# Attention ahead of two MoE layers: four raw buffers, one rotary table, and a start time of its own for every step

## The chip, the cores and the metric

The kernel runs on one core of one Trainium2 chip. The metric is device time in microseconds (us) from launch to end; three runs of the kernel before gave 1014.96 us as their median (1010.65 to 1017.69).

## The reference, cut to what matters

Inputs are q, k and v of shape (4, 8, 576, 64): 4 batches, 8 heads, 576 positions, 64 features, all float32.

- Attention: q and k are turned by rotary tables (`x1*cos - x2*sin`, `x1*sin + x2*cos`), `scores = q_rot @ k_rot.T / 8`, a softmax over the keys (row maximum taken off, exponent, division by the row sum), times v. The result is x with 2304 rows of 512.
- First layer: `h = x @ w_in`, ELU of h, `x = g @ w_out` (2048 hidden columns).
- Second layer: `out = ((x @ w1) * (x @ w2)) @ w3 @ w_out` (1024 hidden columns).

## The kernel before

Attention is done in 16 **units**, one for each batch and pair of heads. The two heads of a unit lie in partitions 0 to 63 and 64 to 127. A TensorE product at float32 accuracy is made of three products of rounded parts (`PAIRS`): a tensor is kept as a high part `hi` and a rest `lo`.

The steps of a unit and the codes that the order uses for them:

- **L1, L0, Lv** (`load`, `load_v`, lines 269 to 275): the loads of k, q and v, issued by SyncE (SP). k and q each come as one tile of 128 x 1152 floats (576 KB): the values and the same values with the two feature halves exchanged. The tiles lie in the pool `qk` (line 237), which has 3 buffers.
- **Km, Ka, Kh, Kl** with w = 1 for k and 0 for q: `turned` multiplies a tile by its table (line 278, GpSimd, POOL), `added` sums its two halves (line 281, POOL), `hi_of` makes the high part (line 289, through line 89, ScalarE, ACT), `lo_of` the rest (line 293, POOL). A raw buffer comes free after Kl.
- **D** (`diagonal`, line 298): two small DMAs that copy the last 64 queries of each head into one tile.
- **SA0 to SA3, SB0 to SB3** (`scores`, line 342): six matmuls each, 128 queries of head A or B against 576 keys. **SC** (`last_scores`, lines 355 to 361): the last 64 queries of both heads in one, with small matmuls of the unit before. Scores lie in PSUM, in a pool of 2 slots (`ps_s`).
- **m** (`maximum`, line 369, VectorE, DVE) and **e** (`exponent`, line 379, ACT): row maximum and exponent of one block. A slot of scores comes free after its e.
- **T, Z** (`turns`, `side_turns`, `last_turns`, lines 390, 410, 420): 88 transposes of 64 x 64 a unit on TensorE (PE), and **E** (lines 426, 428): their copies out of PSUM by ACT or DVE.
- **n, sp, r4** (lines 446 to 454): reciprocals of the sums on DVE, spread by POOL, wanted by the transposes of line 410 and the matmuls of line 356.
- **P0 to P4** (`weigh`, lines 466, 474): the products with v, and **w** (line 486): their normalised result into x.
- **f, W0 to W3** (`fetch_w`, line 103; `weight_step`, lines 499 to 505): 16 tiles of the first layer's weights are fetched (512 KB each) and rebuilt by ACT and DVE.

Work that prepares the first layer (sums of weights, the first splits of x and of a weight set) stands in the last units: `first_sum`, `early_x`, `first_pair`. `early_x` and `first_pair` issue their POOL and ACT steps in one go.

**What sets the order.** All of this lies under a schedule written out by hand. `TIMES` gives each code an offset, unit u takes `u * PERIOD + offset`, `steps` spreads the matmuls of a step by a small distance, and all events are sorted by `max(t, first)` (lines 556 to 648). Only the order counts: each engine runs its own instructions in that order, and each instruction starts when what it depends on is done. Events of the first units that would lie before time zero are clamped (`first=1.75` for L, K and D, zero for the others) and so keep their order among themselves. Two rules follow from the offsets: on SP, D of unit u comes ahead of k of unit u + 2, a weight tile, and q of unit u + 1; on POOL, k of unit u + 2 is turned ahead of q of unit u + 1.

Before the events stands a prologue (lines 621 to 641): the first table and the first tiles of unit 0 in eight pieces on SP (`first_load`, lines 300 to 309; two runs of 288, 128 or 448 floats for each partition), then k of unit 1, `idt`, v of unit 0, and, as the first events, three weight tiles, all ahead of q of unit 1. Unit 0 is turned and split by DVE and ACT (`first_part`). The table of q is loaded on its own and scaled by 1/8 on ACT (line 640). Thirty matmuls on a zero tile keep PE busy while the loads come (`warm_up`).

After attention a planner orders the first layer (`Plan`, lines 668 to 716; products in line 737, lines 780 and 781) by costs and due times of its own, and a fixed loop the second (line 1211 and on).

Of the kernel before, what the change touches and what calls it, by code (L numbers as in the profile page):

```python
# [18 lines left out]
P = 128  # L19
SCALE = 1.0 / 8.0  # L20
# [5 lines left out]
PERIOD = 13.879  # L26
HALF_T = 0.07
TIMES = {
# [12 lines left out]
}  # L41
FIRST_LOADS = ((1, "L1"), (1, "L0"), (2, "L1"))
WARM = 30
# [3 lines left out]
SUM_AT = (7.2, 11.2)  # L47
SWITCH_AT = 15.05
X_AT = (15.06, 15.25, 15.45, 15.65)
PAIR_AT = (15.35, 15.85)  # L50
# [16 lines left out]
def kernel(  # L67
# [161 lines left out]
    with ExitStack() as c1:  # L229
# [7 lines left out]
        qk_p = pool0("qk", 3)  # L237
# [11 lines left out]
        tab = tab_p.tile([P, 2, 2, S], F32, name="tab")  # L249
# [19 lines left out]
        def load(u, w):  # L269
            raws[u, w] = qk_p.tile([P, 2, S], F32, tag="raw_qk", name="raw_qk")  # L270
            nc.sync.dma_start(raws[u, w], (q, k)[w][units[u][0], units[u][1]])
# [4 lines left out]

        def turned(u, w):
            pool.tensor_tensor(raws[u, w], raws[u, w], tab[:, w], op=ALU.mult)  # L278
# [9 lines left out]
        def hi_of(u, w):  # L288
            copy_hi(hl_of(u)[:, w, 0], raws[u, w][:, 0], act)

        def lo_of(u, w):
            hl = hls[u]
            pool.tensor_tensor(hl[:, w, 1], raws[u, w][:, 0], hl[:, w, 0].bitcast(F32), op=ALU.subtract)  # L293

        def diagonal(u):
            for j in range(2):
                h = ROWS[j]
                nc.sync.dma_start(diag[u % 2][h, :, h].bitcast(F32), hls[u][h, 0, :, 512:S].bitcast(F32))

        def first_load():  # L300
            for w in (1, 0):
                raws[0, w] = qk_p.tile([P, 2, S], F32, tag="raw_qk", name="raw_qk")
            for dst, src, a, b in (
                (tab[:, 1], tables[:, 1], 0, 288), (raws[0, 1], k[0, 0], 0, 288),
                (tab[:, 0], tables[:, 0], 0, 128), (raws[0, 0], q[0, 0], 0, 128),
                (tab[:, 1], tables[:, 1], 288, S), (raws[0, 1], k[0, 0], 288, S),
                (tab[:, 0], tables[:, 0], 128, S), (raws[0, 0], q[0, 0], 128, S),
            ):
                nc.sync.dma_start(dst[:, :, a:b], src[:, :, a:b])

        def first_part(w, a, b):
            r, hl, s = raws[0, w], hl_of(0), (SCALE, 1.0)[w]

            def turn(z):
                dve.tensor_tensor(r[:, z, a:b], r[:, z, a:b], tab[:, w, z, a:b], op=ALU.mult)

            def add():
                dve.tensor_tensor(r[:, 0, a:b], r[:, 0, a:b], r[:, 1, a:b], op=ALU.add)

            def high():  # L320
                copy_hi(hl[:, w, 0, a:b], r[:, 0, a:b], act, s)

            def low():
                hi, lo = hl[:, w, 0, a:b].bitcast(F32), hl[:, w, 1, a:b]
                if w:
                    dve.tensor_tensor(lo, r[:, 0, a:b], hi, op=ALU.subtract)
                else:
                    dve.scalar_tensor_tensor(lo, r[:, 0, a:b], s, hi, op0=ALU.mult, op1=ALU.subtract)

            return [lambda: turn(0), lambda: turn(1), add, high, low]  # L330
# [18 lines left out]
        def last_scores(u):  # L349
# [9 lines left out]
            for n in range(2):  # L359
                for i, (a, e) in enumerate(PAIRS):  # L360
                    pe.matmul(
                        s[:, n, :288], diag[u % 2][:, a], hls[u][:, 1, e, n * 288:(n + 1) * 288],
# [3 lines left out]
        def maximum(u, c, j):  # L366
            nm = sm_p.tile([P, 1], F32, tag="nm", name="nm")
            S_t[u, c, j, "m"] = nm
            dve.tensor_reduce(nm, S_t[u, c, j][:, :, :288], axis=AX.XY, op=ALU.max, negate=True)  # L369

        def exponent(u, c, j):
# [3 lines left out]
            else:  # L375
# [4 lines left out]
                p_.rearrange("p (n i) -> p n i", n=2), S_t[u, c, j][:, :, :288], ACTF.Exp,  # L380
# [143 lines left out]
        def first_pair(q):  # L524
            t = set_slot()
            set_pair(0, q, t)
            src = (whole(("i", 0)), sums_of[0][0])[q]
            high_of(t, src)
            rest_of(t, src, pool)

        def early_x(k):
            xf_sum(0, k, pool)
            xf_high(0, k)
            xf_rest(0, k, pool)
# [21 lines left out]
        for code, t_ in TIMES.items():  # L556
            eng = {"a": act, "d": dve}[code[-1]] if code[0] == "E" else None
            for u in range(NU + 3):
                t = u * PERIOD + t_
                if code[0] == "S" and code[1] in "AB":  # L560
                    c = int(code[2])
                    if IN(u):
                        steps(t, scores(u, c, "AB".index(code[1])), 0.133)
                elif code == "SC":
                    if u <= NU:
                        event(t, last_scores, u)
                elif code[0] == "T":
                    du, c = HOST[int(code[2])]
                    if IN(u + du):
                        steps(t, turns(u + du, c, int(code[1])), HALF_T)  # L570
                elif code[0] == "Z":
                    c, l = int(code[2]), int(code[1])
                    v_ = u - (c < 3)
                    if IN(v_):
                        steps(t, last_turns(v_, l) if c == 2 else side_turns(v_, int(c == 1), l), HALF_T)
                elif code[0] == "P":
                    c = int(code[1])
                    v_ = u - (0, 0, 1, 1, 2)[c]
                    if IN(v_):
                        event(t, weigh, v_, c)  # L580
                elif code[0] == "m" and IN(u):
                    event(t, maximum, u, int(code[1]), int(code[2]))
                elif code[0] == "e" and IN(u):
                    event(t, exponent, u, int(code[1]), int(code[2]))
                elif code[0] == "E" and IN(u):
                    f, args = {
                        "X": lambda: (turned_out, (u, int(code[2]), 0)), "Y": lambda: (turned_out, (u, int(code[2]), 1)),
                        "Z": lambda: (side_out, (u, int(code[2]), int(code[3]))), "C": lambda: (last_out, (u, int(code[2]))), "4": lambda: (side4_out, (u,)),
                    }[code[1]]()
                    event(t, f, *args, eng)  # L590
                elif code[0] == "w" and IN(u) and (u, code) != (NU - 1, "w2"):
                    event(t, weighed, u, int(code[1]))
                elif code[0] == "n" and IN(u):
                    event(t, norm, u, *((0, 4), (4, 9))[int(code[1])])
                elif code[:2] == "sp" and IN(u):
                    event(t, spread, u, int(code[2]))
                elif code == "r4" and IN(u):
                    event(t, spread4, u)
                elif code[0] == "W" and u < len(PRE):
# [813 lines left out]
```

## Time and profile before

| | |
|---|---|
| median of 3 runs | 1014.96 us |
| the profiled execution | 1014.97 us |
| span of its instructions | 1013.2 us |
| PE busy | 964.7 us (95%) |
| DVE busy | 758.6 us (75%) |
| ACT busy | 652.1 us (64%) |
| POOL busy | 200.1 us (20%), nearly all in the first 30% of the span |
| mean granted PE clock | 0.979 |

The span runs from the first instruction to the last; the profiled execution has 1.77 us more than that around it. Busy PE is not PE at its peak: the ends of matmuls are modelled, and two that overlap count once.

### The profile page before, as it was taken

The numbers are of one execution on the slowest core, as the hardware profiler recorded it, in microseconds if no ns is written. First come the engines' busy times: TensorE is split into PE (matmuls) and PEld (weight loads), VectorE is DVE, ScalarE is ACT, GpSimd is POOL, SyncE is SP. The second block draws the span as 40 slices with busy tenths as digits, with TensorE's granted clock in tenths as the row PEclk, the third lists the DMA queues.
The fourth block names the chain that finished last, engine by engine and source line by source line (L and its number), as shares of the span: only waits on it lengthen the run. The fifth ranks groups of instructions, "written<-read, shape, count | busy, mean of one in ns | idle before, by whom it ended". The sixth has DMA issues, their size and how long they took to land.

```text
span 1013.2 us, 20015 instructions
## 1 busy us (share of the span) xinstructions
PE 964.7 (95%) x7692; PEld 870.4 (86%) x7692; DVE 758.6 (75%) x1463; ACT 652.1 (64%) x1406; POOL 200.1 (20%) x168
## 2 busy tenths in 40 slices
PE   4599999989989999999999999999999999999998
PEld 3477787878868999999999998998899999999997
DVE  4377777868858999999889999774747576676544
ACT  1477777867867778888778877774544354444432
POOL 1768687777450000000000000000000000000000
PEclk8599999999999999999999999999999999999999
DMA  7242424252410454657564576534142243224311
GB/s 246 86 157 104 170 92 172 96 164 90 156 51 1 141 171 152 218 181 240 192 198 157 191 232 228 179 102 138 40 130 74 73 144 90 84 74 135 90 36 63
DMA packets 65775, 135.19 MB, mean 133 GB/s; under 512 B 11280, under 2 KB 20624, under 8 KB 65680
## 3 DMA queue, kind: packets, MB, share of 16 engines
q1 hardware_dynamic: 65680, 133.92, 40.7%
q8 instruction: 60, 0.98, 0.4%
q14 instruction: 35, 0.29, 0.1%
HBM read 107.15 MB, written 25.69 MB: 131 GB/s over the span
## 4 chain that ended last, share of the span: by engine, by line
PE 75%; POOL 8%; DMA 8%; DVE 3%; ACT 2%; issue 2%; SPq 1%; POOLq 0%; DVEq 0%; ACTq 0%
PE y L780 13%; PE A L1211 10%; PE A L737 9%; PE o L1237 9%; PE B L1211 7%; PE B L737 7%; PE yb L781 7%; PE w L1141 4%; DMA raw_qk<-q_ 4%; POOL raw_qk L278 4%; DMA raw_qk<-k_ 3%; PE o L466 3%; PE s L342 2%; POOL raw_qk L281 1%; POOL hl L293 1%
## 5 line engine op out<-in xcount | busy, mean ns | idle before, releaser
L780 PE MATMUL y<-g,wo 128*128 128x512 f32 x576 | 204.1, 392 | 0.0
L781 PE MATMUL yb<-g,wo 128*128 128x256 f32 x576 | 161.2, 280 | 0.0
L342 PE MATMUL s<-hl 64*128 64x288 f32 x768 | 134.6, 323 | 24.6 <-ACT pr L379 24.3
L369 DVE TENSOR_REDUCE nm<-s 128x1 f32<-128x576 f32 x144 | 108.6, 755 | 62.8 <-PE s L342 50.2
L342 PEld LDWEIGHTS s<-hl 64*128 64x128 f32 x768 | 109.5, 194 | 43.6 <-ACT pr L379 31.7
L148 DVE TENSOR_TENSOR set<-set 128x512 fp32r<-128x512 f32 (+1 forms) x160 | 98.2, 619 | 43.8 <-ACT set L145 43.7
L780 PEld LDWEIGHTS y<-g,wo 128*128 128x128 f32 x576 | 107.8, 187 | 20.5
L379 ACT ACTIVATE pr<-s,nm 128x576 f32<-128x576 f32 x144 | 106.7, 741 | 25.8 <-DVE nm L369 23.9
L1211 PE MATMUL A<-xc,set 128*128 128x384 f32 x576 | 116.1, 336 | 0.2
L737 PE MATMUL A<-xf,set 128*128 128x384 f32 x552 | 111.2, 336 | 1.0 <-DVE p L797 0.9
L1237 PE MATMUL o<-W,g 128*128 128x512 f32 x432 | 111.1, 393 | 0.0
L1211 PEld LDWEIGHTS A<-xc,set 128*128 128x128 f32 x576 | 102.4, 188 | 7.8 <-DVE p L1298 1.0
L781 PEld LDWEIGHTS yb<-g,wo 128*128 128x128 f32 x576 | 108.7, 189 | 0.0
L737 PEld LDWEIGHTS A<-xf,set 128*128 128x128 f32 x552 | 93.7, 188 | 4.3 <-DVE p L797 1.3
L89 ACT ACTIVATE g<-p 128x384 fp32r<-128x384 f32 x48 | 25.2, 526 | 107.8 <-DVE p L1298 71.5
L278 POOL TENSOR_TENSOR raw_qk<-raw_qk,tab 128x1152 f32<-128x1152 f32 x30 | 79.3, 2646 | 66.7 <-DMA raw_qk<-k_ 52.4
L145 ACT ACTIVATE set<-set 128x512 fp32r<-128x512 f32 (+1 forms) x160 | 89.5, 568 | 3.7 <-DMA set<-kept 3.4
L1237 PEld LDWEIGHTS o<-W,g 128*128 128x128 f32 x432 | 80.0, 188 | 12.7
L1211 PE MATMUL B<-xc,set 128*128 128x384 f32 x432 | 86.5, 334 | 0.0
L737 PE MATMUL B<-xf,set 128*128 128x384 f32 x420 | 84.3, 336 | 0.0
L1211 PEld LDWEIGHTS B<-xc,set 128*128 128x128 f32 x432 | 75.9, 188 | 0.0
L737 PEld LDWEIGHTS B<-xf,set 128*128 128x128 f32 x420 | 72.6, 188 | 1.0
(214 smaller groups left out, 1914.0 us busy)
## 6 DMA issues: line engine op xcount, KB each, us to landing
set<-kept SPq DMA_DIRECT2D x120, 256.0 KB, 2.7
raw<-w_ SPq DMA_DIRECT2D x32, 512.0 KB, 4.3
kept<-wr SPq DMA_DIRECT2D x40, 256.0 KB, 3.2
raw_qk<-k_ SPq DMA_DIRECT2D x15, 576.0 KB, 4.2
raw_qk<-q_ SPq DMA_DIRECT2D x15, 576.0 KB, 6.4
raw<-w_in_ SPq DMA_DIRECT2D x16, 512.0 KB, 4.8
raw<-w_out_ SPq DMA_DIRECT2D x16, 512.0 KB, 4.8
w<-kept SPq DMA_DIRECT2D x24, 256.0 KB, 3.5
```

The source lines that it names most:

```text
L145: act.activation(t[:, 0, :w], t[:, 1, :w].bitcast(F32), ACTF.Copy)
L148: eng.tensor_tensor(t[:, 1, :w], t[:, 1, :w].bitcast(F32), t[:, 0, :w].bitcast(F32), op=ALU.subtract)
L278: pool.tensor_tensor(raws[u, w], raws[u, w], tab[:, w], op=ALU.mult)
L342: pe.matmul(S_t[u, c, j][:, n, :288], hl[h, 0, a, c * P:c * P + P], hl[h, 1, e, n * 288:(n + 1) * 288], start=(i == 0), stop=(i == 2),)
L369: dve.tensor_reduce(nm, S_t[u, c, j][:, :, :288], axis=AX.XY, op=ALU.max, negate=True)
L379: act.activation(p_.rearrange("p (n i) -> p n i", n=2), S_t[u, c, j][:, :, :288], ACTF.Exp, bias=S_t.pop((u, c, j, "m")), accum_out=sums[u ...
L737: pe.matmul(banks[b][:, :HF], set_w(n, k, a, c), x[:, e, c], start=(start and i == 0), stop=i == 5, skip_group_check=True,)
L780: pe.matmul(y_t[p, o], w_, g[:, c, :512], start=s, stop=t, skip_group_check=True)
L781: pe.matmul(yb_t[p, o // 2][:, o % 2], w_, g[:, c, 512:], start=s and o % 2 == 0, stop=t, skip_group_check=True,)
L1141: pe.matmul(ps, w3_t[i, j // 4][:, a, j % 4 * P:j % 4 * P + P], wo[j][:, c], start=(j == 0 and n == 0), stop=(j == 7 and n == 2), skip_gro ...
L1211: pe.matmul(ps[:, :HB], w[:, a, c * P:(c + 1) * P], x[:, c, b], start=(start and i == 0), stop=i == 5, skip_group_check=True,)
L1237: pe.matmul(outs[p, o], g[:, a, o % 3 * P:o % 3 * P + P], wW[f][:, c], start=(f == 0 and i == 0), stop=(f == NG - 1 and i == 2),)
```

## The change

- `qk` has 4 buffers in place of 3.
- Inputs q, k and the table are laid out in memory by halves: for each partition the first 288 positions of both parts, then the last 288, so that a half of a tile is one run of 2304 bytes. Tiles have the shape `[P, 2, 2, 288]` (half, part, position). `added`, `hi_of` and `lo_of` read one part as two runs of 288.
- One table is loaded in place of two (the queries of the second head are now in the rotated order of the keys, so `scores` shifts its columns by 64 for it and `diagonal` takes the first 64 columns of it). The table of q is made from it by one ACT instruction (`tab0`).
- `first_load`: the two halves of the table are issued by ACT, the halves of q and k by SP. Then follow k of unit 1, `idt`, q of unit 1, v of unit 0, one weight tile, and k of unit 2. Weight tiles two and three come after L0 of unit 2.
- `first_part`: q of unit 0 is multiplied and summed by POOL, k by DVE. An exponent on one column at the very start is ACT's first instruction after its two DMAs.
- `TIMES`, `PERIOD`, the clamp and the fixed places of the last steps give way to `STARTS`, a list of times for each code, one per unit. `early_x` and `first_pair` are cut into their single steps (`x`, `y`), `first_sum` too (`b`). Eight copies out of PSUM change sides between ACT and DVE, four and four of the same sizes.
- 26 matmuls in the warm-up in place of 30.

Transposes, matmuls, vector and scalar instructions keep their number and sizes otherwise.

```diff
-PERIOD = 13.879
-HALF_T = 0.07
-TIMES = {
-    "L1": -38.79, "f": -38.18, "Km1": -35.79, "L0": -22.65, "Km0": -18.40, ...
...
+HALF_T = 0.063
+STARTS = {
...
+    "SA0": dict(enumerate((8.98, 21.23, 36.65, 51.41, 65.37, 79.70, 94.04, ..., 208.73, 223.59), 0)),
+    "SB0": dict(enumerate((8.98, 22.75, 37.38, 52.04, 66.10, 80.44, ...), 0)),
+    "SA1": dict(enumerate((11.73, 25.47, 39.87, 54.16, 68.55, 82.88, ...), 0)),
+    "D": dict(enumerate((12.00, 21.83, 34.05, 46.48, 57.95, 72.65, 86.98, ...), 0)),
+    "L0": dict(enumerate((13.20, 21.23, 33.45, 45.88, 59.75, 74.45, 88.78, ...), 2)),
+    "L1": dict(enumerate((19.83, 32.05, 43.78, 59.15, 73.85, 88.18, ...), 3)),
+    "Km1": dict(enumerate((9.57, 25.69, 33.69, 45.88, 58.78, 72.99, 87.33, ...), 1)),
+    "Km0": dict(enumerate((13.92, 21.23, 38.21, 50.00, 61.44, 75.65, 89.99, ...), 1)),
+    "Kl0": dict(enumerate((19.78, 31.99, 44.43, 55.58, 71.19, 85.53, ...), 1)),
+    "Z11": dict(enumerate((25.47, 39.83, 54.16, 68.55, 82.88, ...), 1)),
+    "T12": dict(enumerate((13.36, 26.68, 42.32, 56.65, 71.04, 85.37, ...), 0)),
+    "y0": dict(enumerate((227.21, 248.85), 0)),
+    "y1": dict(enumerate((231.25, 250.13), 0)),
...
 }
-FIRST_LOADS = ((1, "L1"), (1, "L0"), (2, "L1"))
-WARM = 30
+WARM = 26
...
-        qk_p = pool0("qk", 3)
+        qk_p = pool0("qk", 4)
...
-            pool.tensor_tensor(raws[u, w][:, 0], raws[u, w][:, 0], raws[u, w][:, 1], op=ALU.add)
+            (dve if (u, w, "a") in ON_DVE else pool).tensor_tensor(raws[u, w][:, :, 0], raws[u, w][:, :, 0], raws[u, w][:, :, 1], op=ALU.add)
...
-            copy_hi(hl_of(u)[:, w, 0], raws[u, w][:, 0], act)
+            copy_hi(halves(hl_of(u)[:, w, 0]), raws[u, w][:, :, 0], act)
...
         def first_load():
             for w in (1, 0):
-                raws[0, w] = qk_p.tile([P, 2, S], F32, tag="raw_qk", name="raw_qk")
-            for dst, src, a, b in (
-                (tab[:, 1], tables[:, 1], 0, 288), (raws[0, 1], k[0, 0], 0, 288),
...
-                nc.sync.dma_start(dst[:, :, a:b], src[:, :, a:b])
+                raws[0, w] = qk_p.tile([P, 2, 2, HS], F32, tag="raw_qk", name="raw_qk")
+            for n in range(2):
+                nc.scalar.dma_start(tab[:, 1, n], tables[:, n])
+                for w in ((0, 1), (1, 0))[n]:
+                    nc.sync.dma_start(raws[0, w][:, n], (q, k)[w][0, 0, :, n])
...
-                    S_t[u, c, j][:, n, :288], hl[h, 0, a, c * P:c * P + P], hl[h, 1, e, n * 288:(n + 1) * 288],
+                    S_t[u, c, j][:, n, :HS], hl[h, 0, a, c * P + 64 * j:c * P + 64 * j + P], hl[h, 1, e, n * HS:(n + 1) * HS],
...
-        def early_x(k):
-            xf_sum(0, k, pool)
-            xf_high(0, k)
-            xf_rest(0, k, pool)
+        def early_x(k, s):
+            if s == 0 or s == 1 and k < 2:
+                xf_sum(0, k, pool)
+            if s == 1:
+                xf_high(0, k)
+            elif s == 2:
+                xf_rest(0, k, pool)
...
+        first_load()
+        pool.memset(zero, 0.0)
+        act.activation(warm[:, :1], zero[:, 0], ACTF.Exp)
+        for s_ in sums:
+            pool.memset(s_[:, :, 1:], 1e-9)
+        load(1, 1)
+        nc.sync.dma_start(idt, ident)
+        load(1, 0)
+        load_v(0)
+        fetch_w(PRE[0], w_in[PRE[0][1]])
+        load(2, 1)
```

## Rows read from the trace of the kernel before

**Rows 1.** Stages: us, engines' busy us (instructions), granted clock, DMA share, GB/s.

```profile
9.79:49.51 39.72, 15.50 (x111) 13.05 (x110) 13.32 (x23) 12.51 (x26) 22.09 (x13) 0.57 0.43 157
49.51:263.47 213.96, 201.13 (x3102) 169.85 (x3102) 165.38 (x324) 165.18 (x389) 156.70 (x124) 0.99 0.38 129
263.47:278.66 15.19, 15.19 (x242) 13.00 (x242) 12.76 (x25) 12.61 (x30) 4.50 (x6) 1.00 0.61 193
278.66:311.19 32.53, 27.81 (x391) 22.78 (x390) 16.62 (x34) 18.35 (x43) 15.16 (x13) 0.95 0.12 39
```

**Rows 2.** Chain that ended last, at 8 and at 104 us: start, us, what.

```profile
7.77 7.78 DMA raw<-w_in_
...
104.19 6.80 DMA raw_qk<-q_
```

**Rows 3.** Timeline, unit 0: start, us, engine, line; idle before and its releaser.

```profile
19.01 1.34 SPq L298 DMA_DIRECT2D diag<-hl  x2
...
20.40 0.59 SPq L271 DMA_DIRECT2D raw_qk<-k_  x1
24.74 5.18 POOL L278 TENSOR_TENSOR raw_qk<-raw_qk,tab 128x1152 f32<-128x1152 f32 x2 [8.73 <-issue]
...
31.42 0.68 ACT L89 ACTIVATE hl<-raw_qk 128x576 fp32r<-128x576 f32 x1 [15.23 <-POOL raw_qk L281]
...
32.88 3.16 PE L342 MATMUL s<-hl 64*128 64x288 f32 x12 [20.70 <-ACT pr L379]
```

**Rows 4.** Waits from 0 to 270 us: us in total, times, longest.

```profile
POOL raw_qk L278 <- DMA raw_qk<-k_: 52.4, 14, 11.0
...
PEld z L410 <- POOL rb L93: 14.9, 13, 2.8
```

**Rows 5.** PE timeline from 250 to 265 us, first rows of its groups.

```profile
250.73 0.40 PE L342 MATMUL s<-hl 64*128 64x288 f32 x1
...
252.48 0.69 PE L466 MATMUL o<-pT,v__3218 128*64 128x64 f32 x16
...
253.22 0.27 PE L390 MATMUL x<-idt,pr 64*128 64x64 f32 x1
...
254.62 1.09 PE L466 MATMUL o<-pT,v__3520 128*64 128x128 f32 x16
...
258.84 0.40 PE L342 MATMUL s<-hl 64*128 64x288 f32 x1
...
260.79 1.09 PE L466 MATMUL o<-pT,v__3821 128*64 128x128 f32 x16
261.81 0.66 PE L355 MATMUL s<-idt,pr 128*128 128x64 f32 x4
...
263.47 0.40 PE L342 MATMUL s<-hl 64*128 64x288 f32 x1
...
264.46 1.09 PE L466 MATMUL o<-pT,v__3821 128*64 128x128 f32 x16
```

**Rows 6.** The page's costliest groups: busy us, mean ns of one, idle before.

```profile
L369 DVE TENSOR_REDUCE nm<-s 128x1 f32<-128x576 f32 x144 | 108.6, 755 | 62.8 <-PE s L342 50.2
...
L379 ACT ACTIVATE pr<-s,nm 128x576 f32<-128x576 f32 x144 | 106.7, 741 | 25.8 <-DVE nm L369 23.9
```

**Rows 7.** POOL instructions by tile: ns min/median/max, first and last start.

```profile
L278 POOL TENSOR_TENSOR raw_qk<-raw_qk,tab x30: 2609/2644/2736, 13.3 to 258.3; 128x1152 f32<-128x1152 f32 x30
L281 POOL TENSOR_TENSOR raw_qk<-raw_qk x30: 1396/1423/1453, 30.0 to 262.6; 128x576 f32<-128x576 f32 x30
...
L200 POOL TENSOR_TENSOR xf<-xT,xf x2: 1832/1839/1846, 280.7 to 283.4; 128x768 fp32r<-128x768 f32 x2
```

**Rows 8.** Single microseconds, columns as in the stages above.

```profile
5.00:6.00 1.00, 1.00 (x11) 1.00 (x10) 0.45 (x2) 0.48 (x1) 0.00 (x0) 1.00 0.93 253
...
15.00:16.00 1.00, 0.00 (x0) 0.00 (x0) 0.00 (x0) 0.62 (x2) 1.00 (x1) 0.60 1.02 410
49.00:50.00 1.00, 1.00 (x13) 0.82 (x14) 0.38 (x1) 0.33 (x1) 0.00 (x0) 0.83 0.00 0
```

More of the change, by code (lines that the diff above doesn't have):

```diff
@@ L275, in load_v, with halves @@
             nc.sync.dma_start(vs[u], v[units[u][0], units[u][1]])
+        def halves(x):
+            return x.rearrange("p (n i) -> p n i", n=2)
         def turned(u, w):
-            pool.tensor_tensor(raws[u, w], raws[u, w], tab[:, w], op=ALU.mult)
+            (dve if (u, w, "m") in ON_DVE else pool).tensor_tensor(raws[u, w], raws[u, w], tab[:, w], op=ALU.mult)
         def added(u, w):
-            pool.tensor_tensor(raws[u, w][:, 0], raws[u, w][:, 0], raws[u, w][:, 1], op=ALU.add)
+            (dve if (u, w, "a") in ON_DVE else pool).tensor_tensor(raws[u, w][:, :, 0], raws[u, w][:, :, 0], raws[u, w][:, :, 1], op=ALU.add)
         def hl_of(u):
@@ L317, in add, with first_part, turn @@
+        def first_part(w, n, eng):
+            r, s = raws[0, w][:, n], (SCALE, 1.0)[w]
+            hi, lo = (hl_of(0)[:, w, e, n * HS:(n + 1) * HS] for e in range(2))
+            def turn():
+                eng.tensor_tensor(r, r, tab[:, 1, n], op=ALU.mult)
             def add():
-                dve.tensor_tensor(r[:, 0, a:b], r[:, 0, a:b], r[:, 1, a:b], op=ALU.add)
+                eng.tensor_tensor(r[:, 0], r[:, 0], r[:, 1], op=ALU.add)
             def high():
-                copy_hi(hl[:, w, 0, a:b], r[:, 0, a:b], act, s)
+                copy_hi(hi, r[:, 0], act, s)
@@ L323, in low @@
             def low():
-                hi, lo = hl[:, w, 0, a:b].bitcast(F32), hl[:, w, 1, a:b]
                 if w:
-                    dve.tensor_tensor(lo, r[:, 0, a:b], hi, op=ALU.subtract)
+                    dve.tensor_tensor(lo, r[:, 0], hi.bitcast(F32), op=ALU.subtract)
                 else:
-                    dve.scalar_tensor_tensor(lo, r[:, 0, a:b], s, hi, op0=ALU.mult, op1=ALU.subtract)
-            return [lambda: turn(0), lambda: turn(1), add, high, low]
+                    dve.scalar_tensor_tensor(lo, r[:, 0], s, hi.bitcast(F32), op0=ALU.mult, op1=ALU.subtract)
@@ L332, in slot_of @@
+            return dict(m=turn, a=add, h=high, l=low)
         def slot_of(u, c, j):
@@ L554, in steps @@
                 event(t + i * dt, f)
[L556 to L599, printed above, removed]
-                    event(t, weight_step, u, int(code[1]))
-                elif code[0] == "K" and 0 < u < NU:
-                    w = int(code[2])
-                    event(t, {"m": turned, "a": added, "h": hi_of, "l": lo_of}[code[1]], u, w, first=1.75)
-                elif code == "D" and 0 < u < NU:
-                    event(t, diagonal, u, first=1.75)
-                elif code[0] == "L" and 0 < u < NU:
-                    if (u, code) not in FIRST_LOADS:
-                        event(t, *((load_v, u) if code[1] == "v" else (load, u, int(code[1]))), first=1.75)
-                elif code == "f" and u < len(PRE):
-                    event(t, lambda u=u: fetch_w(PRE[u], (w_in, w_out)[PRE[u][0] == "o"][PRE[u][1]]))
@@ new lines, in each, with runs @@
+        def each(code, f, lo=0, hi=NU):
+            for u, t in STARTS[code].items():
+                assert lo <= u < hi
+                event(t, f, u)
+        def runs(code, f, dt):
+            for u, t in STARTS[code].items():
+                steps(t, f(u), dt)
+        for c in range(4):
+            for j in range(2):
+                runs(f"S{'AB'[j]}{c}", lambda u: scores(u, c, j), 0.133)
+                runs(f"T{j}{c}", lambda u: turns(u + HOST[c][0], HOST[c][1], j), HALF_T)
+                if c:
+                    runs(f"Z{j}{c}", lambda u: last_turns(u - 1, j) if c == 2 else side_turns(u - (c < 3), int(c == 1), j), HALF_T)
@@ new lines @@
+        event(min(min(v_.values()) for c, v_ in STARTS.items() if c[0] in "xy") - 0.001, switch)
+        parts = {}
+        one.enter_context(tc.manual_schedule())
+        first_load()
[9 more added lines that the diff above has]
+        load(2, 1)
@@ new lines @@
+        dve.memset(warm, 0.0)
+        warm_up(WARM)
+        for d in diag:
+            copy_hi(d, zero.to_broadcast([P, 2, P]), pool)
+        pool.memset(mask, 0.0)
+        for h in ROWS:
+            pool.memset(mask[h, h], 1.0)
+        event(STARTS["tab0"][0], lambda: act.activation(tab[:, 0], tab[:, 1], ACTF.Copy, scale=SCALE))
+        event(STARTS["two"][0], lambda: pool.tensor_tensor(two, idt[:, :D], idt[:, D:], op=ALU.add))
+        events.sort(key=lambda e: e[:3])
+        for *_, f, args in events:
+            f(*args)
@@ L1369, in turned, with by_half @@
         return np.ascontiguousarray(x).reshape(B, 4, P, 2, S)
-    def last_first(x):
+    def by_half(x):
         x = x.copy()
         x[..., 64:, :, :] = np.concatenate([x[..., 64:, :, 512:], x[..., 64:, :, :512]], axis=-1)
-        return x
+        x = x.reshape(*x.shape[:-1], 2, S // 2)
+        return np.ascontiguousarray(x.swapaxes(-3, -2))
     def values(x):
```

244 lines of the change are left out of this document (180 added, 64 removed), and 12 rows, old and new, of the table TIMES.

## The prediction

> **What bounds the kernel now.** I read the stages first [rows 1], because the change touches attention alone. Unit 0 takes 39.72 us, the next 13 units 213.96 / 13 = 16.46 each, unit 14 takes 15.19, and unit 15 with the way into the first layer 32.53. From 311.19 on, 702.0 us of the span are matmuls of the two layers; what they multiply stays the same, so I carry them over whole.
>
> Next came the chain of waits, to see who sets the pace where PE is not full. In unit 0 it goes from a weight tile that took 7.78 us to land [rows 2] through its rebuilding to the wait of SP, and on the timeline of that unit the rest can be followed [rows 3]: D of unit 0 is issued only at 19.01, k of unit 2 queues behind it (20.40), and POOL, whose order has k of unit 2 ahead of q of unit 1, starts that pair at 24.74. ACT stands before the high part of unit 1 until 31.42 with ready exponents behind it, and PE comes back at 32.88 after 20.70 us without work. That is a queue order, not a lack of an engine.
>
> In the 13 middle units the chain crosses the load of q, 6.80 us from its issue [rows 2]. POOL waited 52.4 us in 14 times for the loads of k, and PE's transposes waited 14.9 us in 13 times for a small POOL instruction that stood behind a multiplication without data [rows 4]: 1.15 a unit, nearly all of 16.46 - 15.19 = 1.27. Unit 14 has no more tiles to prepare; PE is busy all its 15.19 us [rows 1]. So 15.19 is what PE alone needs with this order.
>
> **The change, part by part.** The written start times are read for the order alone; every time below is from rows.
>
> *First scores.* DVE's first piece now starts in the sixth microsecond, when 590 kB (a piece of table and one of k) have landed, with the queues at 253 GB/s in runs of 1152 bytes; longer runs moved 410 GB/s [rows 8]. 590 kB at 253 GB/s are 2.3 us, which leaves 3.2 us of start and landing. The first scores now need the table's halves, q's first and k's two: 1.47 MB, 3.6 us at the fast rate, 5.8 at the slow one, so 6.8 to 9.0. Multiplication, sum, high part and rest follow, about 2.1 us (estimate: two on 576 and two on 288 columns, by 755 ns for 576 [rows 6]). That is 8.9 to 11.1 against 9.79; 2304 bytes lie between the two lengths of run, and I take 9.8, no gain. Issue from two queues is worth at most the 0.6 us that an issue takes [rows 3], and the DMA engines are 93% busy in that second [rows 8].
>
> The Trainium skill (DMA: Bandwidth & Descriptors, section "Issuing engines are not separate DMA queues") says that transfers started by several engines share the same 16 DMA engines and that only the time of initiating them is saved; by it the second queue would give nothing beyond that issue, and the 93% agree.
>
> *Unit 0.* It is now bound by its two slots of scores: six matmuls, maximum, exponent, then the slot is free. Six matmuls take 0.99 to the next group's first [rows 5], then come 0.755 and 0.741 [rows 6] and some 0.2 for the hops between engines (estimate): 2.7 for each of four pairs, then SC, 1.66 from 261.81 to 263.47 [rows 5]. Sum 12.5. POOL prepares unit 1 meanwhile: q of unit 0 (all landed at 7.5 to 10.2, then 2.1), two multiplications of 2.64, four instructions of 1.42 [rows 7], small ones: ready at 21 to 24, when unit 0 ends. What covers the loads is that all four tiles of units 0 and 1 are issued before the first weight tile and before D; if that failed, the 20.70 us [rows 3] would come back in part.
>
> *PE's clock.* PE is idle about a third of unit 0 (four pairs of 1.75 and an SC of 1.66 in 12.5). After the idle stretch from 12.2 us on the granted clock fell to 1.2 GHz within the sixteenth microsecond, and it came back to 2.4 only in the fiftieth [rows 8], though PE had work from 32.88 on: gaps keep it low. I expect a fall in unit 0 and a return in unit 1, which is full. At half speed the 0.99 of a slot's matmuls grows by some 0.6 (estimate, a part of it is latency), in four pairs 2.5; and some 4 us of unit 1 at half speed, 2.2. Between nothing and 12 (unit 1 wholly at half speed); 4.7 taken. Unit 0: 15.0.
>
> *Units 1 to 14.* k and q of unit u + 2 are now issued together behind D of unit u, a whole unit before POOL turns them. The fourth buffer allows it: each tile takes the place of its own kind of two units earlier, freed just before D. Landing takes 6.8 us of some 15, so the wait for loads goes, and with it the late small instructions [rows 4]. What is late next? POOL needs 2 x 2.64 + 4 x 1.42 + 1.1 = 12.1 a unit [rows 7]; DVE was busy 12.76 and ACT 12.61 of 15.19 in unit 14 [rows 1], and the eight copies that change sides are of equal sizes. PE ends last, so its order decides. Its five groups of scores and transposes took [rows 5]: 6 matmuls with 8 transposes 0.99 (263.47 to 264.46), 12 with 16 1.75 (250.73 to 252.48), 6 with 16 1.40 (253.22 to 254.62), and two of 12 with 24, one of them 1.95 (258.84 to 260.79). The new order has four: SB0 moves ahead of P1, SB1 into the group of SA1. 0.99 + 1.40 = 2.39 become one more group of 12 with 24, so 1.75 to 1.95, a gain of 0.44 to 0.64; one of the other groups now begins with eight transposes alone, 0.2 by the difference of 1.95 and 1.75. Unit: 15.19 - 0.64 + 0.2 to 15.19 - 0.44 + 0.2, taken 14.85; 14 units 207.9. The ends are 14.5 and 15.19. A two-run read of 288 in Ka, Kh and Kl costs nothing: POOL took 1.84 us for 768 columns in two runs of 384, 2.4 ns a column, and 1.42 for 576 in one run, 2.5 [rows 7].
>
> *Unit 15 and the way into the first layer.* 32.53 now, of which PE stood 4.7 idle, and the clock was 0.95 on average [rows 1]: 5% of 32.5 at half speed, 1.6. POOL's splits and sums of x, 15.16 us in this stretch [rows 1], were issued in one go ahead of what unit 15 needs; single placing takes them from its path. They must still be done before the first product, and the split of the first weight set comes last. 32.53 - 6.1 = 26.4; between 25 and 30 (POOL's 15 us begin late in the unit).
>
> *Sum.* 9.8 + 15.0 + 207.9 + 2.2 + 26.4 = 261.3 against 311.19: 49.9 off. 1013.2 - 49.9 = 963.3, and 1.77 around the span: 965. The profiled execution, 1014.97, stands on the median of the runs, 1014.96, so no shift is due.
>
> **Rivals.**
>
> 1. *Loads still set the pace*, and the change doesn't do what its four buffers say: SP stands at D or at a weight tile whose buffer is not free, and k and q behind it come late, as in rows 4. Units 2 to 14 stay at 16.46: 13 x 1.6 = 21 more, 986. Against it: a unit of slack against a landing of 6.8. Chance 0.09.
> 2. *The clock stays low through units 0 and 1.* As in the stage from 9.79 to 49.51, at 0.57 on average [rows 1]. Some 12 to 14 more: 978. For it speaks that it did so there; against it, that unit 1 is full. 0.14.
> 3. *All goes at the edge*: no fall of the clock, units at 14.5, first scores at 9: 965 - 4.7 - 4.9 - 0.8, about 954. 0.12.
> 4. *Slower than before: POOL becomes the bound.* If the two-run form slowed its four instructions of 576 a unit, POOL's 12.1 us would pass PE's 14.85 from 2.1 us an instruction on, and eat all 49.9 (3.6 a unit) at 3.0. At 3.4 a unit takes 20.0: 14 x 5.2 = 72 more, 1037. Against it stand the 2.4 ns a column [rows 7]. 0.02.
> 5. *POOL and DVE hinder one another at the start*, where both now multiply from SBUF side by side. If DVE's pieces of k waited for POOL's 1.4 and 0.7 on each half, the first scores would come up to 4 us later: 969. The rows show no such pair. Inside the range of the forecast; 0.1 of its chance.
>
> The Trainium skill (GPSIMD Engine Reference, its specification table) has GpSimd's SBUF interfaces shared with VectorE, with contention where a DVE instruction has two SBUF inputs; that is rival 5. No run so far shows its size.
>
> **How the numbers follow.** The forecast (955 to 975, with rival 5) has 0.61, the others 0.14 (978), 0.12 (954), 0.09 (986) and 0.02 (1037), and 0.02 is left for a cause not seen. The range from 952 to 981 takes in rivals 2 and 3 and the bounds of first scores, units and tail, not all of them at once; it leaves out rival 1, rival 4 and the far end of 3. A measurement of this kernel can tell about 1% from no change. Faster by more than that, below 1005, are all cases but rival 4 and half of the unseen one: 0.95. Within 1%: 0.02. Slower: 0.03.
>
> **What the profile after would show.** First scores between 9 and 11; no idle PE of many microseconds before 25; SC every 14.6 to 15.0 us from unit 2 on, and no wait of POOL on a load of k or q there. A clock below 0.9 between 13 and 30 us would bear out the price of the clock, 1.00 throughout would refute it. The first product of the layers near 261; from there 702 to the end. I am wrong in the main step if the middle units still take over 16, or if POOL's instructions on 576 columns take 2 us or more.

## The result and the profile after

The changed kernel takes 975.6 us (median of four runs, 974.46 to 977.05) against 1015.6 of the kernel before beside it: ratio 0.961, 95% interval 0.957 to 0.965. The forecast was 965 (952 to 981). The four runs are two near 974.5, at a mean granted clock of 0.991, and two near 976.9, at 0.985. The profiled execution took 976.7 and is one of the second two; 974.9 of it are span, 38.3 less than before, and PE is busy 98% of that.

Helpers have moved in the file: `turned` is line 377, `added` 380, `lo_of` 392, `scores` 438, `maximum` 465, `exponent` 475; unit 0 has its own lines 412 (multiply), 415 (sum), 422 (rest of k) and 424 (rest of q).

The stages, with the columns of [rows 1]: unit 0, unit 1, units 2 to 13, unit 14, unit 15 with the way to the first product.

```profile
11.46:31.26 19.80, 14.63 (x103) 13.10 (x102) 12.91 (x17) 11.07 (x25) 14.05 (x10) 0.58 0.56 192
31.26:49.60 18.34, 18.29 (x229) 15.49 (x228) 14.32 (x27) 12.61 (x31) 13.44 (x11) 0.81 0.43 140
49.60:230.13 180.53, 180.27 (x2882) 156.96 (x2880) 153.06 (x301) 150.52 (x361) 151.73 (x119) 1.00 0.42 140
230.13:245.79 15.66, 15.57 (x250) 13.37 (x248) 12.85 (x26) 12.70 (x31) 4.91 (x6) 1.00 0.30 97
245.79:270.96 25.17, 24.20 (x384) 20.95 (x383) 16.54 (x35) 18.66 (x43) 11.65 (x11) 1.00 0.32 106
```

A middle unit takes 180.53 / 12 = 15.04 us, and PE is busy all of it. From the first product at 270.96 to the end are 703.9. POOL's waits up to 270 us, beside [rows 4]: no load of k or q is left after the first ones.

```profile
POOL hl L392 <- ACT hl L185: 19.0, 15, 2.9
...
POOL r L550 <- DVE recip L543: 17.1, 12, 7.3
POOL rb L189 <- DVE recip L543: 13.4, 14, 4.9
...
POOL raw_qk L377 <- ACT tab L746: 4.2, 1, 4.2
```

At the start the loads are faster than before: 336 to 419 GB/s in single microseconds from 3 to 7 us, where the shorter runs had 220 to 278. Yet the first scores came late. The timeline there, all engines:

```profile
8.69 2.01 POOL L412 TENSOR_TENSOR raw_qk<-raw_qk,tab 128x576 f32<-128x576 f32 x1 [0.24 <-DMA raw_qk<-q_]
...
9.47 1.54 DVE L415 TENSOR_TENSOR raw_qk<-raw_qk 128x288 f32<-128x288 f32 x1
...
11.63 2.82 POOL L377 TENSOR_TENSOR raw_qk<-raw_qk,tab 128x1152 f32<-128x1152 f32 x1
11.91 4.44 DVE L422 TENSOR_TENSOR hl<-raw_qk,hl 128x288 fp32r<-128x288 f32 x2
14.53 1.50 POOL L380 TENSOR_TENSOR raw_qk<-raw_qk 128x576 f32<-128x576 f32 x1
...
14.82 1.09 PE L438 MATMUL s<-hl 64*128 64x288 f32 x6 [2.97 <-DVE hl L422]
```

DVE's two rests of k, 288 columns each, end 0.3 us behind POOL's two instructions on unit 1, which end at 14.45 and 16.03, and PE waits for them. In single microseconds the granted clock fell at the end of PE's wait and stayed low until the thirty-ninth:

```profile
14.00:15.00 1.00, 0.18 (x2) 0.18 (x4) 1.00 (x2) 0.00 (x0) 0.92 (x2) 0.75 0.00 0
15.00:16.00 1.00, 0.91 (x6) 0.56 (x6) 1.00 (x1) 0.00 (x0) 1.00 (x2) 0.50 0.00 0
37.00:38.00 1.00, 1.00 (x9) 0.39 (x7) 0.00 (x0) 0.64 (x2) 1.00 (x1) 0.50 0.58 168
...
39.00:40.00 1.00, 1.00 (x25) 0.93 (x25) 0.94 (x2) 0.47 (x2) 1.00 (x1) 1.00 0.01 4
```

### The profile page after: what moved, and what is told of

It is laid out like the page before. It is cut to its first block, busy times and chain, and to the rows that moved or that the text cites. A ratio compares the mean times of both kernels' runs of the same rounds, so it can differ in the third digit from the quotient of the medians.

```text
span 974.9 us, 19966 instructions
## 1 busy us (share of the span) xinstructions
PE 958.8 (98%) x7684; PEld 872.3 (89%) x7684; DVE 762.8 (78%) x1455; ACT 650.2 (67%) x1407; POOL 206.8 (21%) x172
## 4 chain that ended last, share of the span: by engine, by line
PE 93%; DVE 3%; ACT 1%; DMA 1%; POOL 1%; issue 1%; POOLq 0%; SPq 0%; DVEq 0%; ACTq 0%
PE y L881 14%; PE A L1312 10%; PE A L838 10%; PE o L1338 10%; PE B L1312 7%; PE B L838 7%; PE yb L882 7%; PE o L562 7%; PE s L438 7%; PE w L1242 4%; PE y L486 2%; PE x L486 2%; PE o L570 1%; PE s L457 1%; PE s L451 1%; PE z L506 1%
## 5 line engine op out<-in xcount | busy, mean ns | idle before, releaser
L438 PE MATMUL s<-hl 64*128 64x288 f32 x768 | 123.7, 322 | 5.8 <-DVE hl L422 3.5
L438 PEld LDWEIGHTS s<-hl 64*128 64x128 f32 x768 | 104.4, 196 | 23.3 <-ACT pr L475 10.5
L465 DVE TENSOR_REDUCE nm<-s 128x1 f32<-128x576 f32 x144 | 106.5, 753 | 19.0 <-PE s L457 8.2
```

The source lines that it names most:

```text
L438: pe.matmul(S_t[u, c, j][:, n, :HS], hl[h, 0, a, c * P + 64 * j:c * P + 64 * j + P], hl[h, 1, e, n * HS:(n + 1) * HS], start=(i == 0), sto ...
L465: dve.tensor_reduce(nm, S_t[u, c, j][:, :, :HS], axis=AX.XY, op=ALU.max, negate=True)
```

## The experiments: where the gain came from

Three kernels start from the kernel before and put in one part at a time. Times are medians of four to ten runs, beside 1015.4 to 1018.3 for the kernel before.

**Four buffers alone.** `pool0("qk", 3)` becomes `pool0("qk", 4)` in the kernel before.

> The kernel before with four buffers for q and k and nothing else changed. Theory (the buffer alone gives nothing, because the written order still has POOL turn k right behind its load): POOL's 52 us of waits for k and the 16.5 us of a middle unit stay, and the time is 1010 to 1017. Rival (the transfers of before were held by their buffers): units fall to 15.2 to 15.8 and the time to 998 to 1006.

Measured: 1015.9, ratio 1.000 (0.998 to 1.002). POOL's waits are what they were:

```profile
POOL raw_qk L278 <- DMA raw_qk<-k_: 52.2, 14, 11.2
```

The buffer alone is worth nothing.

**POOL comes to k one unit later.**

```diff
-    ... "Km1": -35.79, ...
+    ... "Km1": -21.91, ...
```

> The kernel before with one number changed: POOL turns the k of a unit one period later (-21.91 instead of -35.79), at the same place between its neighbours; three buffers, short runs and the periodic order stay. Theory (what the change takes out of the middle units is POOL's wait for a load that was only just issued, so its place in POOL's order pays): the 52 us of waits for k go, the small instructions behind are in time, a middle unit falls from 16.46 to 15.2, 13 x 1.25 = 16 us, and as q of unit 1 no longer stands behind k of unit 2 some 3 to 8 us of the first 49.5 go too: 991 to 997. Rival (POOL's wait moves to the load of q, or the fourth buffer and the new places of the matmuls are what pays): 1005 to 1015.

Measured: 1001.9, ratio 0.987 (0.984 to 0.990): 13.7 faster, where the theory had 18 to 24 and the rival none to 10. Its stages up to unit 13, and the wait that is late next:

```profile
10.89:38.45 27.56, 14.14 (x112) 12.54 (x112) 12.75 (x22) 11.96 (x25) 17.21 (x11) 0.57 0.58 212
38.45:248.37 209.92, 202.46 (x3101) 171.67 (x3101) 165.13 (x324) 164.14 (x389) 161.70 (x127) 0.98 0.39 131
```

```profile
POOL raw_qk L278 <- DMA raw_qk<-q_: 27.1, 14, 3.6
```

Unit 0 falls from 39.72 [rows 1] to 27.56, since q of unit 1 no longer stands behind k of unit 2 on POOL. The middle units stay at 209.92 / 13 = 16.15: POOL's wait for k went, and one for q came, 27.1 us in 14 times, with its small instructions again late behind it. The rival had the mechanism of the middle units right; of the 12 us of unit 0 the theory had 3 to 8, the rival none.

Of PE's 20.70 us without work [rows 3], 12.64 are left here. ACT still stands before the high part of unit 1, now until 23.51, with the first exponent of unit 0 behind it, whose maximum was ready at 18.05. ACT and PE on the timeline of this kernel:

```profile
23.51 0.68 ACT L89 ACTIVATE hl<-raw_qk 128x576 fp32r<-128x576 f32 x1 [7.58 <-POOL raw_qk L281]
24.10 0.72 ACT L379 ACTIVATE pr<-s,nm 128x576 f32<-128x576 f32 x1
```

```profile
24.96 3.17 PE L342 MATMUL s<-hl 64*128 64x288 f32 x12 [12.64 <-ACT pr L379]
```

In the kernel after, the first exponent (18.08) stands ahead of the high part of unit 1 (23.22). No run changed that order on ACT by itself.

**The load of q a unit earlier as well, with the fourth buffer.**

```diff
-    "L1": -38.79, ... "Km1": -35.79, "L0": -22.65, ...
+    "L1": -38.79, ... "Km1": -21.91, "L0": -38.70, ...
-        qk_p = pool0("qk", 3)
+        qk_p = pool0("qk", 4)
```

> The kernel before with four buffers for q and k, POOL's multiplication of k one period later (-21.91) and the load of q one unit earlier, right behind that of k (-38.70 instead of -22.65); short runs at the start, the periodic order of the matmuls and the last unit stay. Theory (with k turned later, POOL's wait moved to the load of q, issued only just before its use; the fourth buffer pays once that load may go out a unit ahead): POOL waits for neither k nor q in the middle units, each takes 15.2 instead of 16.2, 12 to 13 us below the kernel with k moved alone: 988 to 991. Rival (the new order of PE's groups and of the small instructions is what brings the units to 15.05): units stay at 16 and the time at 1000 to 1004.

Measured: 987.7, ratio 0.971 (0.968 to 0.973). All stages:

```profile
10.58:38.19 27.61, 14.26 (x112) 12.44 (x111) 13.01 (x22) 12.30 (x26) 19.50 (x12) 0.57 0.63 230
38.19:235.59 197.40, 196.87 (x3102) 168.09 (x3102) 165.30 (x324) 163.75 (x389) 159.90 (x125) 1.00 0.41 136
235.59:250.78 15.19, 15.19 (x241) 12.99 (x240) 12.75 (x25) 12.59 (x30) 4.49 (x6) 1.00 0.63 194
250.78:284.68 33.90, 29.59 (x392) 23.60 (x391) 16.83 (x34) 18.32 (x43) 15.11 (x13) 0.90 0.12 38
```

The time is just below the theory's 988 to 991, and its mechanism holds: each middle unit now takes 197.40 / 13 = 15.18, the 15.19 that unit 14 needs with nothing to wait for. So two numbers and a buffer, in the old order of PE, bring 27.4 us of span (1013.2 to 985.8) of the 38.3 that the whole change brought. Whether three buffers would do here was not run. The other 10.9 us of the change lie, stage by stage, in unit 0 (27.61 to 19.80) and in unit 15 with the way (33.90 to 25.17), less 5.6 that the start, units 1 to 14 and the layers lose against this kernel. Which of the other edits brought them (the new order on ACT and PE, the single steps at the end of attention, the long runs, the single table) was not tried one by one.

**Three buffers in the new order.** `pool0("qk", 4)` becomes `pool0("qk", 3)` in the kernel after.

> Three buffers for q and k instead of four, in the new order; all else as in the kernel after. Theory 1 (the fourth buffer is what pays): the load of q stands on SP until POOL has made the low part of k of the unit before, lands after POOL wants it, and the middle units go back to 16 us and more: 988 to 998. Theory 2 (the order pays, because POOL now turns a tile about one unit later than before): q waits for its buffer by some 10 us on SP, lands about when POOL comes to it, and a unit loses 0 to 0.3 us; with the start, where SP stands at q of unit 1 with v and a weight tile behind it, 976 to 982.

Measured: 978.4 (975.70 to 979.06), 2.8 above the kernel after by the medians, though the runs of the two overlap; the profiled spans are 2.1 apart. Units 1 and 2 to 13, and the wait that is new:

```profile
30.84:51.56 20.72, 18.62 (x229) 15.71 (x229) 14.29 (x27) 12.51 (x31) 15.78 (x11) 0.82 0.49 166
51.56:232.22 180.66, 180.39 (x2882) 157.04 (x2881) 153.21 (x301) 150.65 (x361) 151.12 (x118) 1.00 0.44 145
```

```profile
PE s L457 <- DMA diag<-hl: 2.0, 1, 2.0
```

The middle units lose nothing (180.66 / 12 = 15.06). The loss lies in unit 1 (20.72 against 18.34): SP stands at a load of q until 44.12, D of unit 1 goes out behind it at 44.50, and PE waits 2.0 us for D. Theory 2 holds: with POOL's turn one unit later, the fourth buffer covers the start alone.

## The experiments: where 10 us stayed

**POOL held back at the start.** In the kernel after, a one-column POOL instruction that reads the end of k's rest stands ahead of Km1 of unit 1:

```diff
+        def hold():
+            x = hls[0][:, 1, 1, S - 1:].bitcast(F32)
+            pool.tensor_tensor(junk, x, x, op=ALU.add)
...
+        event(9.56, hold)
```

> POOL may start the multiplication of k of unit 1 only when DVE has written the low part of k's second half (a one-column POOL instruction that reads that part stands ahead of it); all else as in the kernel after. Theory (POOL's work slows DVE where both take two operands from SBUF): DVE's two low parts of k, 4.44 us together in the kernel after, fall to 0.5 each, the twelve matmuls of the first scores end at 13 to 14 us instead of 17.26, the first scores of unit 1 start 2 to 4 us earlier than 31.26, and the median is 972 to 974. Rival (DVE is held by ACT's high parts or by the loads, not by POOL): the 4.44 stays, first scores stay at 17, POOL is 2 us later with unit 1, and the time is 976 to 978.

Measured: 970.2 (969.75 to 972.34), 5.4 below the kernel after and 2 below the theory's 972 to 974. Timeline of DVE, POOL and PE (the rests are line 428 here):

```profile
12.05 0.81 DVE L428 TENSOR_TENSOR hl<-raw_qk,hl 128x288 fp32r<-128x288 f32 x2
```

```profile
12.94 0.19 POOL L383 TENSOR_TENSOR junk<-hl 128x1 f32<-128x1 f32 x1 [1.13 <-DVE hl L428]
13.09 2.62 POOL L377 TENSOR_TENSOR raw_qk<-raw_qk,tab 128x1152 f32<-128x1152 f32 x1
```

```profile
12.55 0.93 PE L444 MATMUL s<-hl 64*128 64x288 f32 x10 [0.15 <-DVE hl L428]
```

4.44 us became 0.81, by nothing but POOL's later start, and the first scores of unit 1 came at 27.27 instead of 31.26. This settles the cause of the late start.

**PE kept busy.** Matmuls that nobody reads: 16 more in the warm-up, and 17 in five places of unit 0, in the free bank `o`.

```diff
-WARM = 26
+WARM = 42
...
+        for t, n in [(10.0, 4), (14.0, 3), (16.1, 3), (19.5, 3), (20.5, 4)]:
+            event(t, filler, n)
```

> Matmuls that nobody reads keep PE busy: 42 instead of 26 ahead of the first scores, and 17 more in five places of unit 0, in the bank of the weighted sums, which is unused until then; all else as in the kernel after. Theory (the half clock from 14.7 to 38.2 us costs what the forecast had too little of): the granted clock stays near 1.00 through unit 0, its pairs of scores take 2.7 us each instead of 3.52 and unit 1 takes 15.5 instead of 18.1, together 5 to 6 us: 970. Rival (the pairs are set by maximum and exponent, which don't depend on PE's clock): the fillers stand ahead of real matmuls and the time is 975 to 978 whatever the clock.

Measured: 972.5 (971.97 to 972.97), 3.1 below the kernel after, where the theory had 5 to 6; in its profiled execution 3.7. Units 0 and 1:

```profile
14.70:28.71 14.01, 13.01 (x137) 11.77 (x136) 9.64 (x17) 10.43 (x23) 10.02 (x8) 1.00 0.70 234
28.71:44.35 15.64, 15.54 (x230) 13.45 (x229) 13.51 (x27) 12.43 (x30) 13.80 (x11) 1.00 0.56 177
```

The clock is 1.00 throughout, with DVE held by POOL as before. Unit 1 starts at 28.71 instead of 31.26 (2.6) and takes 15.64 instead of 18.34 (2.7). Half speed cost the profiled execution of the kernel after 5.2 us up to there; 1.5 of it was lost again behind attention, where the layers took 705.4 instead of 703.9, for a cause that stays open.

**The table scaled earlier.** `"tab0"` moves from 12.42 to 10.90, ahead of the first exponent on ACT.

> ACT scales the second half of the table ahead of the first exponent instead of behind the second; all else as in the kernel after. Theory (POOL's wait of 4.23 us for it lies beside PE's work, which never waited for unit 1's tiles): POOL's wait goes, q of unit 1 is turned 3 to 5 us earlier, and the median stays within 1 us of 975.6. Rival (the lateness of POOL is passed on to unit 1 by its small instructions): 2 to 4 us faster, 972 to 974.

Measured: 974.6 (974.56 to 975.09), within 1 us as the theory had it. The wait of 4.23 is gone, and unit 0 is no shorter (19.99). The profiled execution gained 2.2 in unit 1 all the same, because the clock came back in the thirty-second microsecond instead of the thirty-ninth. That can't be put down to the edit: in the next kernel, whose order differs from the kernel after only behind unit 14, unit 1 took 16.39 instead of 18.34.

**The end on DVE.** Two rests of the first weight sets, three rests and one difference of x go to DVE, behind its last copies; their places in `STARTS` move with them.

```diff
-            xf_sum(0, k, pool)
+            xf_sum(0, k, dve if k == 2 else pool)
...
-            xf_rest(0, k, pool)
+            xf_rest(0, k, pool if k == 0 else dve)
...
-                rest_of(pair_0[q], src, pool)
+                rest_of(pair_0[q], src, dve)
```

> The kernel after with four of POOL's splits and sums of x and the two rests of the first weight sets behind unit 15 given to DVE, in DVE's order behind its last copies; all else the same. Theory (the end of attention is bound by POOL, 1.82 us for 768 columns where DVE takes 0.95): PE's 1.61 us of wait in the first product goes and the first products run closer, 2 to 4 us: 972 to 974. Rival (DVE's last copies come late behind the splits, so PE gets its last weighted sums later): 975 to 978.

Measured: 972.3 (972.08 to 972.79), 3.3 below the kernel after. The first products of the kernel after, and of this one, on PE:

```profile
270.96 0.61 PE L838 MATMUL C<-xf,set 128*128 128x384 f32 x2
273.18 1.05 PE L838 MATMUL C<-xf,set 128*128 128x384 f32 x4 [1.61 <-POOL set L251]
```

```profile
269.07 1.33 PE L838 MATMUL C<-xf,set 128*128 128x384 f32 x6
270.24 1.20 PE L838 MATMUL B<-xf,set 128*128 128x384 f32 x6
```

PE's wait for POOL's rest of a set is gone; from the first product on are 701.9 instead of 703.9. Those 2.0 are the edit's, the rest is unit 1, 1.95 shorter in the profile, where the clock came back earlier.

**Load of q of unit 1 behind D**, as before the change: `load(1, 0)` moves to an event at 12.01.

> The kernel after with the load of q of unit 1 behind D of unit 0 on SP, as in the kernel before, instead of ahead of v and the first weight tile; all else as after. Theory (all tiles of units 0 and 1 ahead of D is what covers the start): D goes out at 15 to 16, q lands 4 to 6 us behind it, just when POOL comes to it, with the next weight tile beside it; 0 to 3 us slower than 975.6. Rival 1 (SP's order at the start is what cost unit 0 its 20.70 us of idle PE): 10 us or more slower. Rival 2 (no difference, since POOL comes to q of unit 1 only at 20.8): 975 to 976.

Measured: 976.5 (975.65 to 979.40). POOL waited 8.3 us for q, issued behind D at 20.25 by SP, and unit 1 began at 32.45 instead of 31.26. The 0.9 between the medians does not stand out of the runs' spread; rival 1 is refuted.

**All together**, with the hold, fillers of 6, 3, 3, 3 and 4 matmuls (warm-up 26), the early table and the end on DVE.

> The kernel after with POOL held back until k's low parts are written, 19 matmuls that nobody reads in five places of unit 0 (none more ahead of the first scores), the second half of the table scaled ahead of the first exponent, and the end of attention on DVE. Theory (start, clock and end are separate losses): 5 for the hindrance, 3 for the clock, 2 to 3 for the end: 963 to 966. Rival (the clock's loss in unit 1 is the same that the held POOL already gave back, and the end is bound elsewhere): 968 to 971.

Measured: 966.6 (966.40 to 966.73), ratio 0.951 (0.949 to 0.953): faster than both, 9 us below the kernel after and just outside the theory's 963 to 966. Units 0 and 1, and unit 15 with the way:

```profile
11.69:25.67 13.98, 13.46 (x141) 12.23 (x141) 10.31 (x19) 10.88 (x24) 12.77 (x10) 1.00 0.65 226
25.67:41.33 15.66, 15.54 (x231) 13.45 (x230) 13.53 (x27) 12.47 (x30) 14.22 (x11) 1.00 0.61 200
...
237.63:262.79 25.16, 24.19 (x384) 20.93 (x382) 21.13 (x42) 18.62 (x43) 5.42 (x7) 1.00 0.33 106
```

**DVE alone at the start**, two tries on top of it. First q's first half and both halves of k on DVE, POOL held until k is done and then given q's second half:

```diff
-                eng = dve if w == "k" else pool
+                eng = pool if w + n == "q1" else dve
...
-WARM = 26
+WARM = 21
```

> The combined kernel with all of unit 0's first halves on DVE alone, POOL idle until k's low parts are written and then q's second half, and 21 instead of 26 matmuls of warm-up; all else as in the combined kernel. Theory (any two-operand work of POOL beside DVE costs DVE more than it gives): sums on DVE take 0.46 instead of 0.94 and 1.54, the first scores end at 11.5 to 12.3 instead of 13.3, and the time is 1 to 2 us below 966.6: 965. Rival (POOL is late with q's second half and with unit 1, or DVE alone is too slow for two tiles): 966 to 969.

Measured: 972.4 (966.90 to 972.60), so the theory's 965 failed. The start itself was right: sums in 0.46, first scores at once and whole.

```profile
8.94 0.46 DVE L421 TENSOR_TENSOR raw_qk<-raw_qk 128x288 f32<-128x288 f32 x1
...
10.93 1.05 PE L444 MATMUL s<-hl 64*128 64x288 f32 x12
...
15.40 1.56 PE L444 MATMUL s<-hl 64*128 64x288 f32 x8 [1.88 <-ACT pr L481]
```

But ACT stood at the high part of q's second half with the first exponent behind it until 14.53; PE had a gap of 1.88 us, and the clock was 0.62 in 15 to 18 us and 0.50 in 18 to 27. The four runs put a price on such a fall, though one alone was traced: a run with a mean granted clock of 1.000 took 966.90, the other three 972.4 to 972.6 at 0.993. Then ACT's order put right (`pq1h` to 11.75, `pq1l` to 11.90, `tab0` to 12.00):

> The kernel with DVE alone at the start, and on ACT the first two exponents ahead of the high part of q's second half and of the scaled table (DVE's rest of that half behind them too); all else the same. Theory (the earlier first scores were lost because ACT stood 3.25 us for POOL's second half of q with the first exponent behind it, PE had no work from 13.5 to 15.4 and its clock fell to half): the first exponent starts at 12.8 instead of 14.53, PE is idle less than 0.5 us there, the clock stays at 1.00 through unit 0, and the time is 964 to 966.5, at or 2 us below the combined kernel's 966.6. Rival (the second half of q now comes late for the third pair of scores, and the idle time and the fall come there): 968 to 973.

Measured: 971.0 (970.78 to 972.67). The exponent starts at 12.37, and the gap is elsewhere, as the rival said: DVE's rest of q is held by POOL's Km1, and PE waits for it; the clock went to 0.50 at 18.2, two us after that wait, until 28.5.

```profile
13.29 2.64 POOL L377 TENSOR_TENSOR raw_qk<-raw_qk,tab 128x1152 f32<-128x1152 f32 x1
...
14.29 1.96 DVE L430 SCALAR_TENSOR_TENSOR hl<-raw_qk,hl 128x288 fp32r<-128x288 f32 x1 [1.29 <-ACT hl L185]
...
16.30 0.40 PE L444 MATMUL s<-hl 64*128 64x288 f32 x1 [1.47 <-DVE hl L430]
```

The kernel with all four edits stays the fastest.

## Why the prediction was right, and where it was off

The main step held: the wait for loads left the middle units, and PE ended last in them. Behind the sum were the first product at 261.3 and a span of 963.3; measured are 270.96 and 974.9. The 11.6 between, step by step:

- **First scores and unit 0: +6.5** (unit 1 at 31.26, forecast 24.8). The step that failed is rival 5, priced at "up to 4 us", left out of the sum and held to a tenth of the forecast's chance. POOL's work on unit 1 cost DVE's rests of k 3.6 us (4.44 to 0.81), and unit 1's start 4.0. I had named multiplications side by side; it was the rests, which stood against POOL's next unit, that I had not laid beside them. The sums lost another 0.5 and 1.1 (0.94 and 1.54 against 0.46), and DVE alone had its first scores out at 10.9, inside the bounds of 8.9 to 11.1 but not at the 9.8 taken (the 2.1 us in those bounds are 2.27 by their own terms). With the clock up and POOL held, the first scores came at 11.69 and unit 0 itself took 13.98 against 12.5, so that unit 1 began at 25.67, 3.4 later than 9.8 + 12.5; why unit 0 is 1.5 longer stays open. The clock added 1.6 there (27.27 against 25.67) where I had 2.5: 3.4 + 4.0 + 1.6 - 2.5 = 6.5.
- **The clock: term about right.** It fell before 16 us and was low through unit 0 and two fifths of unit 1; 4.7 forecast, 5.2 measured by the fillers for the profiled execution, and some 2.4 less in the runs near 974.5. My reason for a late return, that gaps keep the clock low, the trace does not bear out: PE was busy 19.95 of the 20 us from 19 to 39, and the clock was at 0.50 until the thirty-ninth.
- **Unit 1: +1.3**, of which 0.8 is the unit itself (15.64 against 14.85) and the rest the clock.
- **Middle units and unit 14: +3.1.** 15.04 instead of 14.85: the four groups of scores and transposes take 1.96, 1.93, 1.96 and 1.74 (the first two in the rows below), 7.59 in all, against 0.99, 1.75, 1.41, 1.75 and 1.94, 7.84, for the five of unit 14 before. That is 0.25 gained, where I had 0.34: of the two old groups that I took at 1.95 one took 1.75. The other matmuls of the unit shown, which takes 15.02, need 0.08 more. Unit 14, where the splits of x now stand, took 15.66.

The first rows of two of the four groups and of what follows them, on PE in a middle unit of the kernel after:

```profile
94.74 0.40 PE L438 MATMUL s<-hl 64*128 64x288 f32 x1
...
96.70 1.09 PE L562 MATMUL o<-pT,v__1112 128*64 128x128 f32 x16
...
98.16 0.39 PE L438 MATMUL s<-hl 64*128 64x288 f32 x1
...
100.09 0.69 PE L562 MATMUL o<-pT,v__811 128*64 128x64 f32 x16
```

- **Unit 15 and the way: -1.2** (25.17 against 26.4, where the 6.1 taken off should have been 4.7 + 1.6 = 6.3), and **the layers: +1.9**, PE's wait for POOL's rest of a weight set, which I had carried over as unchanged.

Sum 6.5 + 1.3 + 3.1 - 1.2 + 1.9 = 11.6. The range of 952 to 981 held by its width, which had room for a hindrance of that size; the working of the start was wrong.

Two reasons in it were wrong though the sum held. "The fourth buffer allows it": in the new order three buffers cost 2 to 3 us, all of it in unit 1; what pays is that POOL comes to a tile a unit later and that q's load goes out with k's. And "if that failed, the 20.70 us would come back in part": q of unit 1 loaded late put unit 1 1.2 us later in the profile and cost nothing clear of the spread. The old idle time came from the order of the engines: 8.1 of the 20.70 went with POOL's order alone, k of unit 2 ahead of q of unit 1. The other 12.64 ended only when ACT had made the high part of unit 1 and then the exponent; that the new order on ACT took these away is read from the two timelines and not shown by a run. Rivals 1 and 4 are refuted: no wait for loads, and POOL's two-run sum took 1.41. Rival 2's time of 978 lay near, its mechanism was in the forecast, and the miss came from rival 5.

The Trainium skill (SBUF — State Buffer, section "SBUF: two separate sides") says that a VectorE instruction with two SBUF operands and a GpSimd instruction that reads SBUF want the same port pair, an exclusive lock that is held for a whole instruction while the other is fully blocked. By that the trace agrees: DVE's first rest of k began at 11.91, inside POOL's multiplication, and took 2.86 of the 4.44 us, until just past that one's end at 14.45; and DVE's maxima, which read PSUM, took 1.42 for two beside the same POOL instruction in the kernel with POOL held. Laid beside each other so, the 2.64 and 1.42 of [rows 7] are 4.1 us on the path (estimate), and a tenth of the chance was too little for it.

## What to carry to other kernels

When a wait for a load sits on an in-order engine, look first at where its consumer stands in that engine's order: turning the tile a unit later and issuing both loads a unit ahead, with the buffer for it, brought 27 of 38 us of span, the buffer by itself nothing. Lay every two-operand POOL instruction beside what DVE does from SBUF at that time, across units too, and hold POOL back where DVE is on the path. A gap of one or two microseconds on PE early in a kernel costs more than itself when the clock falls after it; dummy matmuls in a free bank are a cheap test and here a cheap cure.

## What the runs showed of the hardware

- A DVE instruction of 0.46 us on two SBUF operands took 0.94, 1.54 or 2.86 beside POOL's; POOL's own 576 columns went from 1.41 to 2.01. DVE's 768 columns took 0.95 alone and 2.00 beside POOL at the end of attention.
- With gaps of 1.5 to 3.2 us in PE's work in unit 0 the granted clock went from 1.00 to 0.50 (1.2 GHz), in the last microsecond of the gap or up to 2 us behind it, and stayed there for 10 to 24 us, though in the kernel after PE was busy 19.95 of the 20 us from 19 to 39. Executions of kernels with the same order up to unit 14 got it back at different times, a difference of 2 us in unit 1.
- The same gap need not bring a fall. PE's wait of 1.6 us in the first product was followed by 0.50 for 3 to 4 us in the kernel after and in the one with POOL held, and by none in the one with fillers; and one run in four of the first kernel with DVE alone had a mean granted clock of 1.000.
- Runs of 2304 bytes came at 336 to 419 GB/s where runs of 1152 had 220 to 278; the loads come from two queues now too, and the two were not tried apart.
